# A transformer block on one core: gate and up as Strassen products, in chunks of 256 columns

## The chip, the core and the metric

The kernel runs on one core of a Trainium2 chip. The core's engines run side by side and meet at semaphores: TensorE (PE; its weight loads are PEld), VectorE (DVE), ScalarE (ACT), GpSimd (POOL), and SyncE (SP), which here only issues DMAs. Matmul results go to PSUM, in eight banks of 128 partitions x 512 fp32 values; everything else is in SBUF. The metric is the device time of one execution in microseconds.

## The reference

```python
h = x + A(layernorm(x))            # x: 2048 x 576
out = h + B(layernorm(h))

def A(x):   # softmax attention, 32 heads of 18, no mask
    q, k, v = split_heads(x @ wqkv)
    return merge_heads(softmax(q @ k.T * 18 ** -0.5) @ v) @ wo

def B(x):   # 576 -> 4608 -> 576
    g, u = x @ w_gate, x @ w_up
    return (gelu(g) * u) @ w_down
```

All tensors are fp32.

## The kernel before

**Splits.** Every large product is made of fp16 parts. A matrix is scaled by a power of two and split into `hi` (the fp16 cast) and `lo` (what is left); a product is then x_hi w_hi + x_lo w_hi + x_hi w_lo, added up in PSUM in fp32. With 576 = 4 x 128 + 64, and the hi and lo of the last 64 stacked in one tile of 128 partitions, a gate or up tile takes 14 matmuls (`products`, `accumulate`, L272). `exponents` finds the power of two: VectorE reduces the matrix to `ac` and `am` (L122, L125), TensorE transposes `am` (L129) and later spreads its maximum over all partitions by a matmul with ones (L136), and VectorE makes the scale `p_s_...` from it (L167, L169).

**Attention.** 32 steps n = 0 to 31 (head group n // 4, query block of 512 rows n % 4), 16 key tiles each. `fill` supplies TensorE with other work inside a step, `side` is work that is taken a piece at a time. In the last three steps the output products with `wo` of blocks 0 to 2 (`wo_block`) are the fill; that of block 3 comes after attention. `wo_block` adds x, normalises the rows (`rstd_of` ends with `nb`, `normed`), splits them and turns them by DMA transposes on SyncE's queue (`turn`, L231) into X, from which the MLP reads.

**MLP.** The 4608 columns go in 9 chunks of 512, the 2048 rows in 4 blocks of 512. For a chunk c and a block b, `gate_up(c, b)` makes four column tiles; for each of them 14 gate and 14 up matmuls of 512 columns, gelu on ScalarE into `ga` (L637, three buffers), the product with up on VectorE (L639), the fp16 cast on ScalarE (L640) and the rest `lo` on VectorE (L641). `down(c, b)` multiplies the result with the chunk of `w_down`, 8 groups of 12 matmuls of 288 columns, each added to the rows `nat` by VectorE (L658). The output product of one block is written behind gate and up of the next. While a chunk is computed, the weights of the next are loaded and split (`split_gate_up`: L243 on ScalarE, L244 on VectorE; `split_down`: L622, L623). GpSimd has only memsets in the MLP.

**Order.** In attention TensorE's order is written out (`manual_schedule(engines={PE})`). Elsewhere the framework's scheduler sets it for every engine. PSUM is used as two pairs of banks for gate and up and four single banks for the rest.

## Time and profile before

| | before |
|---|---|
| time, median of 3 runs (range) | 2936.56 us (2935.16 to 2939.13) |
| span of the profiled execution | 2934.4 us |
| TensorE busy | 2786.3 us (95%) |
| VectorE busy | 1941.8 us (66%) |
| ScalarE busy | 1461.2 us (50%) |
| GpSimd busy | 274.5 us (9%) |

The profiled execution is one more execution; its span runs from the first to the last instruction, so what lies around the span in a timed run is not in it. The busy shares are means over two very different stages: attention, up to about 1,600 us, and the MLP behind it.

### The profile page before, as it was taken

The page shows a single profiled execution, that of the slowest core. Times are in us where ns is not written, and L with a number is a line of the kernel's source. Part 1 is how long each engine was busy: PE and PEld are TensorE (multiplying, and loading weights), DVE is VectorE, ACT ScalarE, POOL GpSimd, SP SyncE. Part 2 cuts the span into 40 slices and gives each one's busy share as a digit, 9 for nine tenths or more (in the row PEclk, how much of TensorE's full clock was granted, in tenths as well). Part 3 has the DMA queues.
Part 4 walks back from the last instruction along what each step waited for, and adds up shares of the span by engine and source line. Part 5 has one row for each costly group of instructions (what it writes and reads, how often), then busy time and mean ns, then how long its engine had stood idle before and what let it go on. Part 6 is the DMA issues. An engine that isn't in the chain of part 4 may idle for free.

```text
span 2934.4 us, 43173 instructions
## 1 busy us (share of the span) xinstructions
PE 2786.3 (95%) x17311; PEld 1174.1 (40%) x17311; DVE 1941.8 (66%) x3505; ACT 1461.2 (50%) x1758; POOL 274.5 (9%) x472
## 2 busy tenths in 40 slices
PE   6999999999999999999887999999999999999999
PEld 3532222222222222222323555555555555555555
DVE  7469999999999999999864725252525252524222
ACT  5217888888888888888666312121212121212111
POOL 0002321211112121211001000000000000000000
PEclk9999999999999999999999999999999999999999
DMA  8121000000000000000134301010101010100001
GB/s 221 48 74 57 1 25 1 26 1 19 7 1 25 1 25 1 26 5 30 33 65 101 111 1 53 1 53 1 53 1 53 1 53 1 53 1 1 1 17 49
DMA packets 105433, 95.13 MB, mean 32 GB/s; under 512 B 65872, under 2 KB 79312, under 8 KB 105232
## 3 DMA queue, kind: packets, MB, share of 16 engines
q1 hardware_dynamic: 100256, 83.81, 10.2%
q0 software_dynamic: 4976, 8.56, 1.0%
q8 instruction: 135, 2.21, 0.3%
q14 instruction: 66, 0.54, 0.1%
HBM read 63.70 MB, written 14.16 MB: 27 GB/s over the span
## 4 chain that ended last, share of the span: by engine, by line
PE 54%; DVE 38%; ACT 4%; DMA 2%; issue 1%; POOL 1%; SPq 0%; ACTq 0%; DVEq 0%; POOLq 0%
DVE mx L428 36%; PE pair L272 31%; PE bank L272 16%; PE bank L472 3%; PE bank L425 2%; ACT WK L468 1%; ACT W L243 1%; ACT V L243 1%; PE bank L485 1%; DMA X<-nat 0%; ACT V L622 0%; PE pair L466 0%; POOL rc L492 0%; DMA WK<-in_A_wqkv_dram 0%; ACT W L622 0%
## 5 line engine op out<-in xcount | busy, mean ns | idle before, releaser
L428 DVE TENSOR_REDUCE mx<-bank 128x1 f32<-128x512 f32 x2048 | 1272.1, 683 | 85.6 <-PE bank L425 85.1
L468 ACT ACTIVATE WK<-pair,p_ex_sc 128x1024 f32<-128x1024 f32 x1024 | 1085.5, 1114 | 228.4 <-PE pair L466 225.2
L472 PE MATMUL bank<-WK,V 128*32 128x512 f32 x4096 | 549.4, 608 | 0.1
L272 PE MATMUL pair<-X,V 128*128 128x512 f16 x2240 | 489.0, 379 | 3.1 <-ACT ga L637 3.1
L272 PE MATMUL pair<-X,W 128*128 128x512 f16 x2128 | 469.0, 379 | 1.5 <-ACT ga L637 1.5
L639 DVE SCALAR_TENSOR_TENSOR ga<-pair,p_hsc,ga 128x512 f32<-128x512 f32 x144 | 107.7, 748 | 502.5 <-PE pair L272 502.5
L272 PEld LDWEIGHTS <-WK 128*128 128x128 f16 x3456 | 338.2, 98 | 93.2
L637 ACT ACTIVATE ga<-pair,p_gsc 128x512 f32<-128x512 f32 x144 | 98.8, 686 | 490.1 <-PE pair L272 490.1
L272 PEld LDWEIGHTS <-W 128*128 128x128 f16 x2296 | 222.8, 98 | 275.6 <-issue 20.8
L425 PE MATMUL bank<-W 54*128 54x512 f16 x1024 | 292.3, 382 | 42.0 <-DVE mx L428 14.9
L272 PEld LDWEIGHTS <-V 128*128 128x128 f16 x2240 | 218.5, 98 | 261.8 <-issue 3.9
L425 PE MATMUL bank<-A 54*128 54x512 f16 x1024 | 282.8, 383 | 37.8 <-DVE mx L428 9.9
L640 ACT CAST WK<-ga 128x512 f16<-128x512 f32 x144 | 88.9, 618 | 449.8 <-DVE ga L639 449.8
L658 DVE SCALAR_TENSOR_TENSOR nat<-bank,p_dsc,nat 128x288 f32<-128x288 f32 x288 | 147.9, 515 | 194.9 <-PE bank L272 194.9
L472 PEld LDWEIGHTS bank<-WK,V 128*32 128x32 f32 x4096 | 81.2, 108 | 421.7 <-issue 393.0
L272 PE MATMUL bank<-V,WK 128*128 128x288 f16 x1920 | 239.0, 286 | 0.0
L272 PE MATMUL bank<-W,WK 128*128 128x288 f16 x1536 | 191.4, 286 | 0.0
L492 POOL TENSOR_TENSOR rc<-WK,minus_one 128x16 f32<-128x16 f32 x32 | 93.6, 2926 | 873.6 <-ACT WK L487 873.6
L466 PE MATMUL pair<-W 56*128 56x512 f16 x1024 | 161.1, 379 | 5.7 <-ACT WK L468 5.4
L466 PE MATMUL pair<-A 56*128 56x512 f16 x1024 | 156.8, 380 | 2.8 <-ACT WK L468 2.6
L425 PEld LDWEIGHTS <-W 54*128 54x128 f16 x1024 | 61.8, 93 | 222.5 <-issue 214.6
L641 DVE TENSOR_TENSOR WK<-ga,WK 128x512 f16<-128x512 f32 x144 | 99.3, 689 | 76.3 <-ACT WK L640 76.1
(160 smaller groups left out, 1281.2 us busy)
## 6 DMA issues: line engine op xcount, KB each, us to landing
V<-in_B_w_down_dram SPq DMA_DIRECT2D x9, 1152.0 KB
A<-in_B_w_gate_dram SPq DMA_DIRECT2D x9, 1024.0 KB
A<-in_B_w_up_dram SPq DMA_DIRECT2D x9, 1024.0 KB
qk_hi<-qk SPq DMA_DIRECT2D x36, 128.0 KB
qk_lo<-qk SPq DMA_DIRECT2D x36, 128.0 KB
A<-in_A_x_dram SPq DMA_DIRECT2D x32, 144.0 KB
out_dram<-nat SPq DMA_DIRECT2D x16, 288.0 KB
WK<-in_A_wqkv_dram SPq DMA_DIRECT2D x3, 1152.0 KB
```

The costliest lines, as they stand in the source:

```text
L272: nc.tensor.matmul(dst, a, b, start=(i == 0), stop=(i == len(pairs) - 1))
L425: nc.tensor.matmul(pms[j][:, :TB], Q[r, q0 : q0 + P], K[r, kc * TB : (kc + 1) * TB], start=True, stop=True)
L428: nc.vector.tensor_reduce(mx[:, t, 2 * pr + j, kc : kc + 1], pms[j][:, :TB], axis=AX.X, op=ALU.max)
L466: nc.tensor.matmul(pS[:, j, :TB], K[r, kt * P : (kt + 1) * P], Q[r, qc * TB : (qc + 1) * TB], start=True, stop=True)
L468: nc.scalar.activation(pes[(2 * kt + pr) % NPE], pS[:, :, :TB], AF.Exp, scale=ex_sc)
L472: nc.tensor.matmul(acc[32 * hh : 32 * hh + 32, :TB], Vg[n // NB][:, kt * G4 + hh * VC : kt * G4 + hh * VC + 32], pes[(2 * kt + hh // 2) % ...
L492: nc.gpsimd.tensor_tensor(rc, den, minus_one.to_broadcast([P, TPB * 4]), op=ALU.pow)
L637: nc.scalar.activation(ga, pg[:, :TB], AF.Gelu_apprx_tanh, scale=gsc)
L639: nc.vector.scalar_tensor_tensor(ga, pu[:, :TB], hsc, ga, op0=ALU.mult, op1=ALU.mult)
L640: nc.scalar.copy(hh[:, f], ga)
L641: nc.vector.tensor_sub(hl[:, f], ga, hh[:, f])
L658: nc.vector.scalar_tensor_tensor(nat[:, t, ws], pt[:, :HALF], dsc, nat[:, t, ws], op0=ALU.mult, op1=ALU.add)
```

## The change

**Strassen.** A gate (or up) product of 1,024 rows (a pair of blocks, p = 0, 1) with 256 columns is cut into 2 x 2: rows into two blocks, columns into two tiles of 128, and the 576 of the sum into two halves of 288. The seven products m1 to m7 of sums and differences replace the eight block products. A half of 288 is 2 x 128 + 32, with the parts of the last 32 stacked, so a product takes seven matmuls of 512 columns (`product`). `quad` writes them in the order m3, m2, m5, m4, m1, m7, m6, and combines them into four results: three copies of products on ScalarE and eight additions or subtractions on VectorE that read PSUM. `gate` then has four gelus; `up` has four products with gate on VectorE, four casts on ScalarE and four subtractions for `lo` on GpSimd.

**Rows.** `pair_rows(p)` normalises the rows of two blocks, makes the seven sums and differences, splits them and turns them by two transposes per tile, of 15 and 20 blocks. For p = 0 it is side work of attention's last step; for p = 1 it runs during up(0,0) and down(0,0).

**Weights.** Chunks have 256 columns, so there are 18. `split_mat` makes the sums and differences of the weights as well: scaling and casts on ScalarE, additions and subtractions on GpSimd, in place of VectorE's share. Gate, up and down have an `exponents` call each. `prepare(0)` is side work of attention.

**Order.** The MLP is written in `manual_schedule()` for all engines: each engine does its instructions in program order. `step(cost)` counts time in the program and takes pieces of the side work by the numbers that they yield. The chunk's order is gate(c,p), down of the pair before, up(c,p). The output product of block 3 (`turn_o(3)`, `wo_block(3)`) stands behind gate(0,0). The eight banks are single: acc0 to acc3 for the products, acc4 to acc6 for down, acc7 for `exponents`.

```diff
@@ -54,9 +54,10 @@
     TB = min(512, S)
     NB = S // TB
     TPB = TB // P
-    FT = 4
+    FT = 2
     FC = FT * P
     NCH = DF // FC
+    NPR = NB // 2
     QK = 2 * D
     NG = H // 4
...
                                         apply_absolute_value=True)
-                yield
+                yield 4
         nc.vector.tensor_reduce(am, ac, axis=AX.X, op=ALU.max)
-        yield
-        pt = next(m_ring)
+        yield 9
+        pt = next(e_ring)
         for i in range(n):
             nc.tensor.transpose(pt[0:1, i * P : (i + 1) * P], am[:, i : i + 1], id32)
+        if spread:
+            yield
         a1 = small.tile([1, n], F32, tag=f"a1{n}", name=f"a1_{name}")
         nc.vector.tensor_reduce(a1, pt[0:1, : n * P].rearrange("o (n p) -> o n p", n=n),
                                 axis=AX.X, op=ALU.max)
         nc.vector.tensor_scalar_max(a1, a1, 2.0 ** -60)
-        yield
-        pb = next(m_ring)
+        yield 7
+        pb = next(e_ring)
         nc.tensor.matmul(pb[:, :n], ones[0:1], a1, start=True, stop=True)
+        if spread:
+            yield
...
+    def turn_o(b):
+        for i in range(TPB):
+            nc.sync.dma_start_transpose(OT[:, :, i * P : (i + 1) * P], nat16[:, b * TPB + i])
+
+    def wo_block(b, each=False):
...
-                run(accumulate(pt[:, :HALF], products(slice(t * P, (t + 1) * P), oh, ol, ws)))
+                k = t - b * TPB
+                run(accumulate(pt[:, :HALF], products(slice(k * P, (k + 1) * P), oh, ol, ws,
+                                                      (OT[:, :NK], OT[:, NK], OT[:, NK + 1 :]))))
                 nc.vector.scalar_tensor_tensor(nat[:, t, ws], pt[:, :HALF], u_o, xb,
                                                op0=ALU.mult, op1=ALU.add)
                 yield
             row_stats(nat[:, t], t)
-        rstd_of(b * TPB, TPB)
...
+            if each:
+                rstd_of(t, 1)
+                yield
+        if not each:
+            rstd_of(b * TPB, TPB)
...
+    def pair_rows(p):
+
+        ys, z = rows[p]
+        for v in ys:
+            nc.gpsimd.memset(v[:, :, HALF + 64 : 3 * P], 0.0)
+        for i in range(TPB):
+            t1, t2 = 2 * p * TPB + i, (2 * p + 1) * TPB + i
+            a, b = slice(0, HALF), slice(HALF, D)
+            for k, t, h in ((6, t1, a), (3, t1, b)):
+                nc.scalar.activation(z[:, k], nat[:, t, h], AF.Identity,
+                                     scale=rs[:, t : t + 1], bias=nb[:, t : t + 1])
+            normed(z[:, 0], nat[:, t2, b], t2)
+            normed(z[:, 2], nat[:, t2, a], t2)
+            yield
+            nc.vector.tensor_add(z[:, 1], z[:, 6], z[:, 0])
+            nc.gpsimd.tensor_add(z[:, 4], z[:, 6], z[:, 2])
+            nc.vector.tensor_add(z[:, 5], z[:, 3], z[:, 0])
+            nc.gpsimd.tensor_sub(z[:, 2], z[:, 2], z[:, 0])
+            nc.vector.tensor_sub(z[:, 3], z[:, 3], z[:, 6])
+            for j, k0, k1 in ((1, KA, 7), (0, 0, KA)):
+                y, zz = ys[j], z[:, k0:k1]
+                yield 5
+                nc.scalar.copy(y[:, :, :HALF], zz)
+                yield 5
+                nc.vector.tensor_sub(y[:, :, 3 * P :], zz[:, :, : 2 * P], y[:, :, : 2 * P])
+                nc.vector.tensor_sub(y[:, :, HALF : HALF + 32], zz[:, :, 2 * P :],
+                                     y[:, :, 2 * P : HALF])
+                nc.scalar.copy(y[:, :, HALF + 32 : HALF + 64], y[:, :, 2 * P : HALF])
+                nc.sync.dma_start_transpose(
+                    XP[p][:, NP * k0 : NP * k1, i * P : (i + 1) * P],
+                    y.rearrange("p a b -> p (a b)"))
+            yield
+
+
...
+    def split_mat(src, s167, parts, name):
+
+        h25, l25, h, l = parts
+        l4 = l.rearrange("p k (c n) -> p k c n", c=2)
+        e = yield from exponents([src.rearrange("p (c a) b -> p c (a b)", c=3)], name)
+        s = pow2(e, -1, 267, f"s_{name}")
+        for i in range(2):
+            v = src[:, 3 * i : 3 * i + 3]
+            nc.scalar.activation(v, v, AF.Copy, scale=s)
+            yield
+        f0, f1 = slice(0, P), slice(P, FC)
+        nc.gpsimd.tensor_add(s167[:, 0], src[:, :3, f0], src[:, 3:, f1])
+        nc.scalar.copy(h[:, 3], src[:, :3, f0])
+        yield 5
+        nc.gpsimd.tensor_sub(s167[:, 1], src[:, :3, f1], src[:, :3, f0])
+        nc.scalar.copy(h[:, 4], src[:, 3:, f1])
+        yield 5
+        nc.gpsimd.tensor_sub(s167[:, 2], src[:, 3:, f0], src[:, 3:, f1])
+        yield 5
+        r = slice(64, R3)
+        for k, v in ((3, src[:, :3, f0]), (4, src[:, 3:, f1])):
+            nc.gpsimd.tensor_sub(l4[:, k], v[:, :2], h[:, k, :2])
+            nc.gpsimd.tensor_sub(h[r, k, 2], v[r, 2], h[r, k, 2])
+            yield 5
+        nc.scalar.copy(h[:, :3], s167)
+        for c in range(3):
+            nc.gpsimd.tensor_add(src[:, c], src[:, c], src[:, 3 + c])
+            yield
+        for k in range(3):
+            nc.gpsimd.tensor_sub(l4[:, k], s167[:, k, :2], h[:, k, :2])
+            yield 4
+        nc.gpsimd.tensor_sub(h[r, :3, 2], s167[r, :, 2], h[r, :3, 2])
+        yield 6
+        nc.scalar.copy(h25, src[:, :3])
+        yield 4
+        nc.gpsimd.tensor_sub(l25, src[:, :2], h25[:, :2])
+        nc.gpsimd.tensor_sub(h25[r, 2], src[r, 2], h25[r, 2])
+        yield 6
+        return e
...
+    def split_down(src, c, eg, eu):
+        dh, dl = slots[c % 2][2:]
+        ed = yield from exponents([src], "dn")
         s = pow2(ed, -1, 268, "s_dn")
-        nc.vector.tensor_add(ed, ed, e[:, 0:1])
-        nc.vector.tensor_add(ed, ed, e[:, 1:2])
+        nc.vector.tensor_add(ed, ed, eg)
+        nc.vector.tensor_add(ed, ed, eu)
         dsc = pow2(ed, 1, -262, "dsc")
         for f in range(FT):
-            nc.scalar.activation(dh[:, f], df[:, f], AF.Copy, scale=s)
-            nc.vector.scalar_tensor_tensor(dl[:, f], df[:, f], s, dh[:, f],
+            nc.scalar.activation(dh[:, f], src[:, f], AF.Copy, scale=s)
+            yield
+            nc.vector.scalar_tensor_tensor(dl[:, f], src[:, f], s, dh[:, f],
                                            op0=ALU.mult, op1=ALU.subtract)
+            yield
...
+        yield
+        yield from after("g", need)
+        e = yield from split_mat(a, sums[0], slots[c % 2][0], "g")
+        kept[c, "g"] = pow2(e, 1, -23, "gsc")
+        if not first:
+            load_mat(b, w_up, c, nc.sync)
+            yield 55
+        yield from after("u", need + (c == 1))
+        kept[c, "h"] = pow2(e, -1, 225, "hsc")
+        eu = yield from split_mat(b, sums[1], slots[c % 2][1], "u")
+        kept[c, "u"] = True
...
+    def product(k, xp, parts):
+
+        h25, l25, h, l = parts
+        if k in (2, 5):
+            fs = slice(P, FC) if k == 2 else slice(0, P)
+            wh, wl = h25[:, :, fs], l25[:, :, fs]
+        else:
+            i = {1: 0, 6: 1, 7: 2, 3: 3, 4: 4}[k]
+            wh, wl = h[:, i], l[:, i].rearrange("p (c n) -> p c n", c=2)
+        x = xp[:, NP * XK[k] : NP * (XK[k] + 1)]
+        r = []
+        for c in range(2):
+            r += [(wh[:, c], x[:, c]), (wh[:, c], x[:, 3 + c]), (wl[:, c], x[:, c])]
+        r.append((wh[:R3, 2], x[:R3, 2]))
+        return r
+
+    sides = []
+
+    def step(cost):
+        ghost["now"] += cost
+        for sd in list(sides):
+            while ghost["now"] >= sd[1]:
+                r = next(sd[0], sd)
+                if r is sd:
+                    sides.remove(sd)
+                    break
+                sd[1] += r or 3
+
+    def begin(it):
+        sides.append([it, ghost["now"]])
+        return sides[-1]
+
+    def quad(xp, parts, tmps, out):
+
+        def mm(k):
+            bank = next(single_ring)[:, :TB]
+            ps_ = product(k, xp, parts)
+            for i, (w, x_) in enumerate(ps_):
+                nc.tensor.matmul(bank, w, x_, start=i == 0, stop=i == len(ps_) - 1)
+            step(7)
+            return bank
...
+        c12, c22, c21, c11 = [temp(tmps) for _ in range(4)]
+        m3 = mm(3)
+        nc.scalar.copy(c12, m3)
+        m2 = mm(2)
+        nc.vector.tensor_sub(c22, c12, m2)
+        nc.scalar.copy(c21, m2)
+        m5 = mm(5)
+        nc.vector.tensor_add(c12, c12, m5)
+        nc.scalar.copy(c11, m5)
+        out(0, 1, c12)
+        m4 = mm(4)
+        nc.vector.tensor_add(c21, c21, m4)
+        nc.vector.tensor_sub(c11, m4, c11)
+        out(1, 0, c21)
+        m1 = mm(1)
+        nc.vector.tensor_add(c11, c11, m1)
+        nc.vector.tensor_add(c22, c22, m1)
+        m7 = mm(7)
+        nc.vector.tensor_add(c11, c11, m7)
+        out(0, 0, c11)
+        m6 = mm(6)
+        nc.vector.tensor_add(c22, c22, m6)
+        out(1, 1, c22)
...
+    def up(c, p, hsc, ga, tmps=up_tmps):
+
+        def out(f, b, v):
+            r = ga[f, b]
+            nc.vector.scalar_tensor_tensor(r, v, hsc, r, op0=ALU.mult, op1=ALU.mult)
+            nc.scalar.copy(hh[:, f, b], r)
+            nc.gpsimd.tensor_sub(hl[:, f, b], r, hh[:, f, b])
+
+        quad(XP[p], slots[c % 2][1], tmps, out)
+        ghost["u"] += 1
...
+        for i in range(2 * TPB):
+            t = 2 * p * TPB + i
+            b, tsl = i // TPB, slice(i % TPB * P, (i % TPB + 1) * P)
...
                         run(fill)
+                        turn_o(qc - 1)
                         fill = wo_block(qc - 1)
+                        if qc == 3:
+                            run(side)
+                            side = pair_rows(0)
...
-    e, gsc, hsc = kept[0]
-    for t in range((NB - 1) * TPB, NT):
-        turn(nat16[:, t], t)
-    for _ in wo_block(NB - 1):
-        pass
-    dsc = split_down(0, e)
-    prev = None
-    for c in range(NCH):
-        for b in range(NB):
-            h = gate_up(c, b, gsc, hsc)
-            if prev is not None:
-                down(*prev)
-            prev = (c, b, h, dsc)
-            if b == 0 and c + 1 < NCH:
-                load_gate_up(c + 1)
-                nx = result(split_gate_up(c + 1))
-                ndsc = split_down(c + 1, nx[0])
-        if c + 1 < NCH:
-            (e, gsc, hsc), dsc = nx, ndsc
-    down(*prev)
+    with tc.manual_schedule():
...
+        begin(rest)
+        ga = gate(0, 0, kept[0, "g"], first_gate)
+        for _ in wo_block(NB - 1):
+            step(5)
+        wait_for(1, "g")
+        rows1 = begin(pair_rows(1))
+        up(0, 0, kept[0, "h"], ga, first_up)
+
+        prev = (0, 0)
+        for c in range(NCH):
+            for p in range(NPR):
+                if (c, p) == (0, 0):
+                    continue
+                if (c, p) == (0, 1):
+                    down(*prev, kept[0, "d"])
+                    while rows1 in sides:
+                        step(1)
+                    ghost["rows"] = 1
+                ga = gate(c, p, wait_for(c, "g"))
+                if (c, p) != (0, 1):
+                    down(*prev, wait_for(prev[0], "d"))
+                wait_for(c, "u")
+                up(c, p, kept[c, "h"], ga)
+                prev = (c, p)
+        down(*prev, kept[NCH - 1, "d"])
 
 
```

On VectorE, before, in the MLP where the next chunk's weights are searched for their maximum (`ac_gu`, `am_gu`; `ac_dn`, `am_dn` for the down weights):

```order
L122 TENSOR_REDUCE ac_gu<-A 128x1 x2
L641 TENSOR_TENSOR WK<-ga,WK 128x512
L122 TENSOR_REDUCE ac_gu<-A 128x1 x3
L122 TENSOR_REDUCE ac_dn<-V 128x1
L125 TENSOR_REDUCE am_gu<-ac_gu 128x2
L122 TENSOR_REDUCE ac_dn<-V 128x1 x2
L639 SCALAR_TENSOR_TENSOR ga<-pair_67,p_hsc,ga 128x512
L122 TENSOR_REDUCE ac_dn<-V 128x1
L641 TENSOR_TENSOR WK<-ga,WK 128x512
L125 TENSOR_REDUCE am_dn<-ac_dn 128x1
L639 SCALAR_TENSOR_TENSOR ga<-pair_67,p_hsc,ga 128x512
```

and now, at the end of up(c,0) (L840 and L843 are `quad`'s last two evictions, L861 is up's product with gate, L735 the `lo` of the down weights, L125 and L128 the reductions for the next gate chunk, L826 the first eviction of gate(c,1)):

```order
L735 SCALAR_TENSOR_TENSOR A<-WK,p_s_dn,A 128x576 x2
L840 TENSOR_TENSOR WK<-WK,acc_12926 128x512
L861 SCALAR_TENSOR_TENSOR WK<-WK,p_hsc 128x512
L125 TENSOR_REDUCE ac_g<-W 128x1
L843 TENSOR_TENSOR WK<-WK,acc_12927 128x512
L861 SCALAR_TENSOR_TENSOR A<-WK,p_hsc,A 128x512
L125 TENSOR_REDUCE ac_g<-W 128x1 x2
L128 TENSOR_REDUCE am_g<-ac_g 128x1
L826 TENSOR_TENSOR ga<-ga,acc_12929 128x512
```

The reductions stood between evictions before too; now two instructions for the down weights and the last evictions of up(c,0) are in front of `am_g`, in a fixed order.

On TensorE, before, at the first products behind a chunk's reductions (L129 transposes `am`):

```order
L272 MATMUL bank_71<-W,WK 128x288
L129 MATMUL bank_69<-id_78,am_gu 1x128 x2
L129 MATMUL bank_68<-id_78,am_dn 1x128
L272 LDWEIGHTS V
L272 MATMUL pair_66<-X,V 128x512
```

and now, in gate(c,1) (acc_12926 is the bank of its third product, acc_12927 that of its fourth):

```order
L818 LDWEIGHTS A
L818 MATMUL acc_12926<-V,A 128x512
L132 MATMUL acc_12933<-id_78,am_g 1x128
L818 LDWEIGHTS A
L818 MATMUL acc_12927<-V,A 128x512
```

The transpose of `am_g` now stands between two products of the same quad, and the fourth waits behind it.

On SyncE, before, from the last blocks' turns on (L231; L568 loads x for the output product, L235 to L237 load weights):

```order
L568 DMA A<-in_A_x_dram 128x288 x8
L231 DMA_TRANSPOSE X<-V 128x9x128 x4
L231 DMA_TRANSPOSE X<-nat 128x9x128 x4
L568 DMA A<-in_A_x_dram 128x288
L237 DMA A<-in_B_w_gate_dram 64x512
L568 DMA A<-in_A_x_dram 128x288
```

and now (L569 is `turn_o(3)`, L630 the transposes of `pair_rows(1)`, L577 loads x, L677 and L679 load weights):

```order
L569 DMA_TRANSPOSE V<-nat 128x9x128 x4
L577 DMA V<-in_A_x_dram 128x288 x4
L677 DMA W<-in_B_w_up_dram 128x2x256
L679 DMA W<-in_B_w_up_dram 128x1x256
L677 DMA W<-in_B_w_up_dram 128x2x256
L679 DMA W<-in_B_w_up_dram 128x1x256
L577 DMA V<-in_A_x_dram 128x288 x4
L630 DMA_TRANSPOSE V<-V 128x15x128
L630 DMA_TRANSPOSE V<-WK 128x20x128
```

The transposes of the second pair, of 15 and 20 blocks, stand behind the loads for the last output product; before, block 3's own turns stood there.

## Rows read from the trace of the kernel before

**Rows 1.** The page, its span and the busy row of TensorE.
```profile
span 2934.4 us, 43173 instructions
...
PE 2786.3 (95%) x17311; PEld 1174.1 (40%) x17311; DVE 1941.8 (66%) x3505; ACT 1461.2 (50%) x1758; POOL 274.5 (9%) x472
```

**Rows 2.** Timeline of TensorE, steady part: start us, us, engine, line, operation.
```profile
1903.66 24.34 PE L272 MATMUL pair<-X,V 128*128 128x512 f16 x112
1927.83 11.92 PE L272 MATMUL bank<-W,WK 128*128 128x288 f16 x96
1939.59 0.38 PE L129 MATMUL bank<-id,am_gu 128*1 128x128 f32 x2
1939.81 0.27 PE L129 MATMUL bank<-id,am_dn 128*1 128x128 f32 x1
...
1941.09 0.38 PE L136 MATMUL bank<-a_gu,ones 1*128 1x2 f32 x2
1941.34 0.36 PE L136 MATMUL bank<-a_dn,ones 1*128 1x1 f32 x2
```

**Rows 3.** Windows: stretch, length, busy us by engine (PE, PEld, DVE, ACT, POOL), clock.
```profile
1609.00:1625.00 16.00, 15.82 (x113) 11.94 (x114) 7.47 (x17) 0.00 (x0) 0.00 (x0) 0.87 0.48 96
2300.00:2400.00 100.00, 99.61 (x578) 56.24 (x577) 44.48 (x90) 22.52 (x35) 1.04 (x2) 1.00 0.12 39
```

**Rows 4.** Timeline of TensorE from attention to MLP; in brackets the idle time before.
```profile
1597.78 1.04 PE L272 MATMUL pair<-X,V 128*128 128x512 f16 x4
...
1609.18 15.83 PE L272 MATMUL bank<-W,X 128*128 128x288 f16 x112 [5.39 <-DMA X<-nat]
1624.85 18.94 PE L272 MATMUL pair<-X,V 128*128 128x512 f16 x87
...
1651.84 0.27 PE L129 MATMUL bank<-id,am_dn 128*1 128x128 f32 x1 [3.08 <-DVE am_dn L125]
```

**Rows 5.** Waits of TensorE from 1,600 us on: us in total, times, longest.
```profile
PE pair L272 <- ACT ga L637: 4.7, 9, 1.1
```

**Rows 6.** Groups by line, whole span: count, busy us, mean ns of one.
```profile
L658 DVE SCALAR_TENSOR_TENSOR nat<-bank,p_dsc,nat 128x288 f32<-128x288 f32 x288 | 147.9, 515 | 194.9 <-PE bank L272 194.9
L639 DVE SCALAR_TENSOR_TENSOR ga<-pair,p_hsc,ga 128x512 f32<-128x512 f32 x144 | 107.7, 748 | 502.5 <-PE pair L272 502.5
L641 DVE TENSOR_TENSOR WK<-ga,WK 128x512 f16<-128x512 f32 x144 | 99.3, 689 | 76.3 <-ACT WK L640 76.1
...
L122 DVE TENSOR_REDUCE ac_gu<-A 128x1 f32<-128x512 f32 x90 | 56.5, 667 | 0.0
...
L622 ACT ACTIVATE W<-V,p_s_dn 128x576 f16<-128x576 f32 x16 | 11.0, 761 | 2.9 <-DVE p_s_dn L169 2.9
...
L169 DVE TENSOR_SCALAR p_s_dn<-pi_s_dn 128x1 int32<-128x1 int32 x9 | 1.4, 152 | 0.2
```

**Rows 7.** Groups of GpSimd, shapes apart: count, busy us, mean ns of one.
```profile
L502 POOL CAST nat<-o 128x288 f16<-128x288 f32 x32 | 14.2, 443 | 1.7
...
L551 POOL TENSOR_TENSOR W<-X,W 128x576 f16<-128x576 f32 x4 | 5.1, 1280 | 0.2
...
L505 POOL TENSOR_TENSOR nat<-o,nat 128x256 f16<-128x256 f32 x4 | 2.7, 668 | 0.0
```

**Rows 8.** Timeline of GpSimd at two of those instructions.
```profile
1551.63 0.98 POOL L502 CAST nat<-o 128x288 f16<-128x288 f32 x1
...
1605.14 0.67 POOL L505 TENSOR_TENSOR nat<-o,nat 128x256 f16<-128x256 f32 x1
```

**Rows 9.** Timeline of VectorE at the first of these moments.
```profile
1551.58 0.75 DVE L244 SCALAR_TENSOR_TENSOR V<-A,p_s_gu,V 128x512 f16<-128x512 f32 x1 [1.67 <-ACT V L243]
...
1629.72 0.16 DVE L209 SCALAR_TENSOR_TENSOR nb<-mv,rs 128x4 f32<-128x4 f32 x1
```

**Rows 10.** Transposes by DMA, SyncE's queue: ns min/median/max, first and last start.
```profile
L231 SPq DMA_TRANSPOSE X<-nat x16: 1287/1372/1557, 1430.4 to 1610.4; - x16
```

**Rows 11.** Timeline of ScalarE at the end of attention.
```profile
1580.55 16.19 ACT L468 ACTIVATE WK<-pair,p_ex_sc 128x1024 f32<-128x1024 f32 x16 [2.03 <-PE pair L466]
```

More of the change, by code (lines that the diff above doesn't have):

```diff
@@ L644, in down, with prepare, after @@
-    def down(c, b, h, dsc):
-        hh, hl = h
-        dh, dl = slots[c % 2][4:]
-        for i in range(TPB):
-            t = b * TPB + i
-            tsl = slice(i * P, (i + 1) * P)
+    def prepare(c):
+        first = c == 0
+        a, b, d = (g0, u0, d0) if first else (g1, g1, dn) if c == 1 else (gn, gn, dn)
+        sums = sums0 if first else [sums1, sumsn] if c == 1 else [sumsn] * 2
+        need = 2 * (c - 1)
+        def after(k, last):
+            while not first and ghost[k] < last:
+                yield
+        if first:
+            load_mat(a, w_gate, c, nc.sync)
+            load_mat(b, w_up, c, nc.sync)
+        if c != 1:
+            load_down(d, c, nc.sync)
+        yield
[3 more added lines that the diff above has]
+        if not first:
+            load_mat(b, w_up, c, nc.sync)
+            yield 55
[3 more added lines that the diff above has]
+        kept[c, "u"] = True
+        if c + 1 < NCH and not first:
+            load_mat(gn, w_gate, c + 1, nc.sync)
+        if c == 1:
+            yield from after("rows", 1)
+            load_down(d, c, nc.sync)
+            yield 20
+        yield from after("d", need)
+        kept[c, "d"] = yield from split_down(d, c, e, eu)
@@ new lines, in preparer @@
+    def preparer():
+        for c in range(1, NCH):
+            yield from prepare(c)
+    def product(k, xp, parts):
[12 more added lines that the diff above has]
+        return r
@@ L693, in tile_block @@
         fill = other_products()
-        side = iter(())
         take(fill, 14)
```

161 lines of the change are left out of this document (93 added, 68 removed).

## The prediction

> **What bounds the kernel now.** I read the page's busy rows first, then TensorE's waits from 1,600 us on, then its timeline, and the other engines only where TensorE waits or will wait. The page shows TensorE busy for 95% of a span of 2934.4 us [rows 1]. In the MLP it is the bound: of the 100 us from 2,300 on it is busy for 99.6 at a granted clock of 1.00 (2.4 GHz), with VectorE at 44.5, ScalarE at 22.5 and GpSimd at 1.0 [rows 3]. Its waits on `ga`, the rotating buffer of gelu results, come to 4.7 us in nine times [rows 5]. So a matmul that goes is worth its full pitch, as long as the others keep up. The pitches come from one steady block [rows 2]: 112 gate and up matmuls fill 1903.66 to 1927.83, which is 0.2158 us each, and 96 output matmuls fill 1927.83 to 1939.59, 0.1225 each. Between attention and MLP TensorE isn't the bound: it waits 5.39 us for a transpose and 3.08 for `am_dn` [rows 4].
>
> **What the change removes.** A Strassen product takes 7 matmuls, so gate and up take 18 x 2 x 2 x 49 = 3528 matmuls in place of 9 x 4 x 4 x 28 = 4032: 504 x 0.2158 = **-108.8 us**. The output products stay at 3456 matmuls. The handover's losses of before go as well, because gate(0,0) now stands where TensorE waited: 5.39 and 3.08 [rows 4], the 4.7 on `ga` [rows 5], and the slow clock of the last output product. Its 112 matmuls took 15.83 where 112 x 0.1225 is 13.7, at a mean clock of 0.87, so part of it at 1.2 GHz after the wait [rows 3, 4]: 2.1. Together **-15.3**.
>
> **What it adds on TensorE.** Each `exponents` call puts a transpose and a matmul with ones into TensorE's row. Two transposes took 0.22 (1939.59 to 1939.81) and one such matmul 0.25 (1941.09 to 1941.34) [rows 2], so a call is about 0.36, and the pair of calls of before about 0.83 (three transposes 0.33, two matmuls 0.50). There will be 51 calls in the MLP for nine pairs: 51 x 0.36 - 9 x 0.83 = **+10.9**.
>
> **The handover.** gate(0,0) waits for the transposes of `pair_rows(0)`, which are issued at the end of attention: +1, an estimate. `turn_o(3)` waits for GpSimd's last subtraction. Before, that ended at 1605.81 [rows 8] and TensorE's first output matmul followed at 1609.18 [rows 4], 3.4 later, a transpose of 1.37 [rows 10] and 2.0 of landing. Counted from 1597.78 [rows 4] this is 11.4, against 49 x 0.2158 = 10.6 of cover, 0.8 over; and GpSimd now has one instruction of the weight split in between, 128x576 in 1.28 [rows 7] at most: **+2.1**. At the end of attention ScalarE is full: 16 exponentials without a gap in 16.2 us [rows 11]. Into this go four tiles of 576, 864 and 1,152 elements for `pair_rows(0)`, 4 x 3.4 = 13.7 by L622 [rows 6], and more for `prepare(0)`. TensorE's filler of before leaves room there, so I take **+3**, with -5 and +15 as bounds (all hidden but the handover, all exposed).
>
> **The second pair of blocks.** gate(0,1) needs `pair_rows(1)`, which needs the last `rstd`. From the start of gate(0,0): 10.6, the 2.1, 13.7 of output product, then 4.8 until `nb` (its end at 1629.88 against the product's at 1625.01 [rows 4, 9]) gives 31.2. Behind it VectorE has, in its written order, four tiles of about 4.7 (five of 288 elements, 768, 1,024 and two small ones, at L641's rate of 689 ns for 512 [rows 6]) = 19.0; the evictions of up(0,0), 8 x 0.689 + 4 x 0.748 = 8.5; those of down(0,0), 16 x 0.515 = 8.2; and the exponents of a matrix, 3 x 0.667 and seven small ones of 0.152, 0.2 with the gap between them = 3.4 [rows 6]. That ends at 70.3. The last tile's casts on ScalarE, 864 and 1,152 elements at L622's rate [rows 6], show about 3; the last transpose has 20 blocks, 3.0 by the 1.37 for nine [rows 10], and lands 2.0 later: 78.3. TensorE's own work until then is 26.4 + 10.6 + 11.8 + 0.4 = 49.2. The stall is 29.1, and the clock after it costs twice the 2.1 of the old, shorter gap, 4: **+33.1**. Bounds: 15, where the tiles spread over both engines without queueing, and 45.
>
> **The steady chunks.** Pure TensorE work is 28 x 7 x 0.2158 + 192 x 0.1225 + 3 x 0.36 = 66.9 us for 256 columns. Before it is (4 x (24.17 + 11.76) + 0.83) / 2 = 72.3 for as many [rows 2]. VectorE's list comes to about 55 of it (32 evictions at 0.689, 8 at 0.748, 32 at 0.515, 6 reductions at 0.667, two of 576, `dl`, small ones at 0.152 [rows 6]); GpSimd's to 33. Neither is the bound by its sum, but both are late at two places that the order shows. First, up(c,0)'s second product reads `l25`, the last thing that GpSimd makes of the up weights. Counted from the start of gate(c,0): `am_u`'s product with ones ends at 10.95, VectorE has `p_s_u` at 13.05 behind evictions, ScalarE scales for 1.75 (768 elements twice, at most 1.01 each by L622 [rows 6], whose mean holds a fixed part), and GpSimd's 11.3 follow (eight of 256 at 0.668, and by the step from there to 576 in 1.28 [rows 7] three of 384 at 0.91, one of 512 at 1.16, and 2 for the small ones): 26.1, where TensorE comes to it at 24.6. That is 1.5 per chunk. Second, the transpose of `am_g` stands three products into gate(c,1), at 39.7 with that wait. VectorE starts up(c,0)'s list at 27.8 and has 14.6 of work ahead of `am_g` (evictions, two reductions of 576, two `dl`, three reductions of 512, ten small ones): 42.4, which is 2.7 more. TensorE takes its instructions in order, so everything behind the transpose waits too. The pattern is fixed from chunk 8 on, ten times: 42.5, and I add 4 for chunks 1 to 7, where the side work drifts past less tight places: **+46.5**. Bounds: nothing, if VectorE's instructions overlap enough when they stand close, and twice that.
>
> GpSimd and VectorE now work at the same time, which the MLP of before hardly shows. At the one place where the trace has both, a cast by GpSimd took 0.98 at 1551.63 [rows 8] against a mean of 0.443 [rows 7], while VectorE's L244, with two inputs from SBUF, ran from 1551.58 for 0.75 [rows 9]. The Trainium skill (SBUF — State Buffer, Who interferes with whom) has a rule for this: a VectorE instruction with two SBUF inputs contends with a GpSimd instruction that reads SBUF, and whichever comes first holds the other off. By that rule the trace agrees here, with 0.54 us lost by the second comer. If it held for all ten such instructions of a chunk, and VectorE came second each time, the sum would be that of rival 2 below; by the row alone, GpSimd pays.
>
> **The sum.** 2934.4 - 108.8 + 10.9 - 15.3 + 1 + 2.1 + 33.1 + 46.5 + 3 = 2906.9 of span. The median of the runs is 2936.56, 2.2 above the profiled span, so the forecast is **2909 us**.
>
> **Rivals.** (1) The steady waits are hidden: VectorE's and GpSimd's instructions overlap enough at their pitches for TensorE never to wait in chunks 8 to 17. For it speaks that their sums are 55 and 33 of 67; against it, the two places where the order is strict. Then 2909 - 46.5 = 2863.
> (2) Slower: VectorE and GpSimd hold each other off. Ten VectorE instructions of a chunk have two inputs in SBUF (eight of up's last step, two of `dl`), and GpSimd is busy for half of it. If each costs the chain of `l25` or of `am_g` the 0.54 seen above, that is 5.4 a chunk, 92 in 17: about 3001. It decides from 33 us, 2.0 a chunk, or four of ten meetings on the path. Against it: one meeting is all the trace has, and GpSimd lost there, not VectorE.
> (3) No change: the four product banks turn over too slowly, because a bank is read by ScalarE and then by VectorE before it is free. At 0.4 us for each of the 68 steady quads' handovers, 27 us go, and 2936 is left. Against it: a product takes 1.51, and its two reads about 0.7 each (L641, 0.689 [rows 6], taken for ScalarE's too), with four banks in turn.
> That the change does not cut the matmuls is no rival: the order shows 3528.
>
> **How the numbers follow.** Forecast 0.45, rival 1 0.25, rival 2 0.20, rival 3 0.10. About 0.2% (5.9 us, so 2930.7 to 2942.4) is what a measurement of this kernel can tell from no change. The forecast's own range is 2885 to 2935, from the bounds of the second pair and of the steady waits; 0.42 of its 0.45 lies below the bound of no change. Faster: 0.42 + 0.25 = 0.67. Same: 0.03 of the forecast, 0.07 of rival 3, 0.02 of rival 2 = 0.12. Slower: 0.18 + 0.03 = 0.21. The range reaches down to rival 1 less some of the attention's and the second pair's bounds, 2856, and up into rival 2 to 2955; rival 2 above that and the lowest corner are left out, under 0.2.
>
> **What would show it.** Gate and up at 0.216 a matmul and 3528 of them. One long wait of TensorE, near 29 us, ahead of gate(0,1), ended by a transpose. From chunk 8 on a period near 71.2 us, with TensorE waiting for GpSimd ahead of up(c,0)'s second product and for `am_g` in gate(c,1). A period of 67 shows rival 1; 72 or more with GpSimd's or VectorE's means above those of before shows rival 2. I am wrong if the first product of many quads waits for a bank, or if attention's last two blocks grow by more than 15 us.

## The result, and the profile after

| | before | after |
|---|---|---|
| time, median of 4 runs | 2935.86 us | 2948.89 us (2943.20 to 2951.72) |
| ratio of the times, 95% interval | | 1.0046 (1.0028 to 1.0063) |
| span of the profiled execution | 2934.4 us | 2941.4 us |

The changed kernel is 13 us slower, where 2909 was forecast. Its profiled execution is the fastest of its four; the spans of the others are 2944.8, 2949.5 and 2949.9.

The page of the changed kernel (span, then busy time, share and count by engine):

```profile
span 2941.4 us, 45089 instructions
...
PE 2714.7 (92%) x16906; PEld 1133.3 (39%) x16906; DVE 2398.9 (82%) x4489; ACT 1712.8 (58%) x2144; POOL 886.1 (30%) x1194
```

TensorE has 72 us less to do than in [rows 1], less than the 108.8 of the matmuls that went, and its share fell from 95% to 92%. From the first gate matmul behind attention to the end, first the kernel before, then the changed one (length, TensorE's busy time, and so on by engine):

```profile
1597.78:2934.40 1336.62, 1319.88 (x7665) 750.16 (x7663) 528.27 (x1029) 265.53 (x411) 12.78 (x22) 1.00 0.09 28
```

```profile
1603.55:2941.40 1337.85, 1249.95 (x7246) 708.46 (x7245) 994.96 (x2018) 497.79 (x765) 595.49 (x706) 0.98 0.13 37
```

TensorE works 70 us less there and stands idle 71 us more (87.9 against 16.7). TensorE's waits from 1,590 us on (in total, times, longest), in the place of [rows 5]:

```profile
PE acc L132 <- DVE am_g L128: 29.8, 11, 3.4
PE acc L818 <- DMA V<-WK: 10.7, 1, 10.7
PE acc L279 <- ACT WK L862: 9.5, 2, 8.3
PE acc L818 <- POOL A L720: 6.7, 5, 1.3
PE acc L818 <- POOL W L720: 6.7, 5, 1.3
PE acc L279 <- DVE nat L881: 6.5, 7, 1.8
```

The first, fourth and fifth are the two steady waits: 2.7 us each for `am_g` (L132 is its transpose), 1.34 each for `l25` (L720). The second, and 8.3 of the third and 5.1 of the sixth, lie between gate(0,0) and gate(0,1). TensorE's timeline from gate(0,0) to gate(1,0), which answers to [rows 4]:

```profile
1603.55 10.76 PE L818 MATMUL acc<-X,A 128*128 128x512 f16 x49 [0.56 <-ACT WK L494]
1616.19 5.32 PE L279 MATMUL acc<-W,V 128*128 128x288 f16 x42 [1.88 <-DMA V<-nat]
...
1643.49 4.87 PE L818 MATMUL acc<-X,A 128*128 128x512 f16 x14 [3.41 <-ACT W L827]
1656.61 0.66 PE L279 MATMUL acc<-A,WK 128*128 128x288 f16 x2 [8.26 <-ACT WK L862]
...
1689.21 21.42 PE L818 MATMUL acc<-V,A 128*128 128x512 f16 x91 [10.73 <-DMA V<-WK]
...
1712.52 1.68 PE L818 MATMUL acc<-X,W 128*128 128x512 f16 x7
```

gate(0,1), at 1689.21, is the first work that needs the second pair's rows (V); it comes 85.7 us after gate(0,0). The steady part, two chunks in the place of [rows 2] (X marks gate(c,0) and up(c,0), V the second pair):

```profile
2200.87 7.74 PE L818 MATMUL acc<-X,A 128*128 128x512 f16 x35
...
2227.20 2.77 PE L818 MATMUL acc<-X,A 128*128 128x512 f16 x12 [1.33 <-POOL A L720]
...
2244.62 0.27 PE L132 MATMUL acc<-id,am_g 128*1 128x128 f32 x1 [2.92 <-DVE am_g L128]
2244.73 4.87 PE L818 MATMUL acc<-V,A 128*128 128x512 f16 x14
...
2275.25 7.74 PE L818 MATMUL acc<-X,W 128*128 128x512 f16 x35
...
2317.99 0.27 PE L132 MATMUL acc<-id,am_g 128*1 128x128 f32 x1 [2.52 <-DVE am_g L128]
2318.10 3.19 PE L818 MATMUL acc<-V,W 128*128 128x512 f16 x14
```

The same 14 matmuls take 3.19 us behind a wait of 2.52 and 4.87 behind one of 2.92. The windows say why (granted clock third from the end):

```profile
2244.00:2248.00 4.00, 3.38 (x11) 1.36 (x12) 2.79 (x8) 2.11 (x4) 1.07 (x1) 0.67 0.01 4
...
2320.00:2324.00 4.00, 4.00 (x20) 1.84 (x19) 3.47 (x9) 1.87 (x4) 0.00 (x0) 1.00 0.01 2
```

Behind the first wait part of the stretch runs at 1.2 GHz, a loss of 1.68 us; behind the second none. It isn't the wait's length alone that decides: of the eleven on `am_g`, which take 2.5 to 3.4, four are followed by such a stretch, at 2095, 2170, 2244 and 2463, with 3.41, 2.51, 2.92 and 2.93. A chunk from 2200.87 takes 74.4, the next ones 71.7 and 72.7.

### The profile page after: what moved, and what is told of

Read it like the earlier page. It is cut to its first block, busy times and chain, and to the rows that moved or that the text cites. A ratio compares the mean times of both kernels' runs of the same rounds, so it can differ in the third digit from the quotient of the medians.

```text
span 2941.4 us, 45089 instructions
## 1 busy us (share of the span) xinstructions
PE 2714.7 (92%) x16906; PEld 1133.3 (39%) x16906; DVE 2398.9 (82%) x4489; ACT 1712.8 (58%) x2144; POOL 886.1 (30%) x1194
## 4 chain that ended last, share of the span: by engine, by line
DVE 45%; PE 41%; POOL 5%; issue 3%; ACT 3%; DMA 2%; SPq 0%; POOLq 0%; DVEq 0%; ACTq 0%
DVE mx L435 36%; PE acc L818 19%; PE acc L279 10%; PE pair L279 4%; PE bank L479 2%; PE bank L432 2%; PE bank L279 2%; DVE ac_g L125 1%; ACT WK L475 1%; POOL W L711 1%; DVE ga L861 1%; DVE nat L881 1%; PE bank L492 1%; DMA V<-nat 0%; DVE A L735 0%
## 5 line engine op out<-in xcount | busy, mean ns | idle before, releaser
L279 PEld LDWEIGHTS <-WK 128*128 128x128 f16 x3456 | 337.6, 98 | 114.3 <-ACT WK L862 10.8
L881 DVE SCALAR_TENSOR_TENSOR nat<-acc,p_dsc,nat 128x288 f32<-128x288 f32 x576 | 295.5, 516 | 103.5 <-PE acc L279 101.9
L432 PE MATMUL bank<-W 54*128 54x512 f16 x1024 | 289.9, 381 | 41.2 <-DVE mx L435 13.5
L818 PEld LDWEIGHTS <-A 128*128 128x128 f16 x1764 | 171.6, 98 | 229.0 <-issue 25.6
L279 PE MATMUL acc<-A,WK 128*128 128x288 f16 x1728 | 219.9, 288 | 14.6 <-ACT WK L862 8.3
L279 PE MATMUL acc<-W,WK 128*128 128x288 f16 x1728 | 218.1, 288 | 4.2 <-DVE nat L881 1.4
L818 PE MATMUL acc<-V,A 128*128 128x512 f16 x882 | 201.2, 385 | 12.1 <-DMA V<-WK 10.7
L818 PE MATMUL acc<-X,A 128*128 128x512 f16 x882 | 199.4, 381 | 10.7 <-POOL A L720 6.7
L818 PE MATMUL acc<-X,W 128*128 128x512 f16 x882 | 197.8, 379 | 6.7 <-POOL W L720 6.7
L818 PE MATMUL acc<-V,W 128*128 128x512 f16 x882 | 199.4, 384 | 0.4 <-DVE WK L840 0.4
L863 POOL TENSOR_TENSOR WK<-ga,WK 128x512 f16<-128x512 f32 x74 | 88.3, 1193 | 220.8 <-ACT WK L862 142.2
L432 PEld LDWEIGHTS <-A 54*128 54x128 f16 x1024 | 60.3, 93 | 214.6 <-issue 208.0
```

The lines of the kernel that those rows point to most:

```text
L279: nc.tensor.matmul(dst, a, b, start=(i == 0), stop=(i == len(pairs) - 1))
L432: nc.tensor.matmul(pms[j][:, :TB], Q[r, q0 : q0 + P], K[r, kc * TB : (kc + 1) * TB], start=True, stop=True)
L818: nc.tensor.matmul(bank, w, x_, start=i == 0, stop=i == len(ps_) - 1)
L863: nc.gpsimd.tensor_sub(hl[:, f, b], r, hh[:, f, b])
L881: nc.vector.scalar_tensor_tensor(nat[:, t, ws], pt[:, :HALF], dsc, nat[:, t, ws], op0=ALU.mult, op1=ALU.add)
```

## The experiments

Ratios are to the kernel before on the same chip; the changed kernel's is 1.0046, and 0.001 is 2.9 us. Differences between two of them are known to about 4 to 7 us.

**One of the steady waits: `l25`.** In `split_mat`:

```diff
+        nc.scalar.copy(h25, src[:, :3])
+        yield 4
+        nc.gpsimd.tensor_sub(l25, src[:, :2], h25[:, :2])
...
         for k in range(3):
             nc.gpsimd.tensor_sub(l4[:, k], s167[:, k, :2], h[:, k, :2])
...
-        nc.scalar.copy(h25, src[:, :3])
-        yield 4
-        nc.gpsimd.tensor_sub(l25, src[:, :2], h25[:, :2])
```

> Only the order inside the weights' split changes: the parts for the second and fifth product (h25, l25) are made before the lo parts of the first, sixth and seventh, so l25 is ready about 2.6 us sooner, against a wait of 1.34. Theory (each of the two waits of a chunk is a cost of its own): the 13.4 us of waits on l25 in ten chunks go, the waits on am_g stay at 29.8, the time falls by 11 to 15 us. Rival (VectorE's list sets the pace, the wait only moves): the waits on am_g grow by what is gained, the time stays within 4 us.

1.0043 (1.0028 to 1.0058): no gain that can be told from noise. Neither reading was right. The waits on `l25` are gone, those on `am_g` are as they were (first row), but the mean clock of 2,200 to 2,800 fell to 0.98 (second):

```profile
PE acc L132 <- DVE am_g L128: 30.2, 11, 3.4
```

```profile
2200.00:2800.00 600.00, 576.74 (x3307) 324.71 (x3305) 455.51 (x921) 228.71 (x349) 278.45 (x333) 0.98 0.10 31
```

0.99 is the changed kernel's value there. The clock was lower in all four executions: 0.980 to 0.983 over the span, against 0.986 and 0.987 for the changed kernel. The early chunks lost as well: chunks 1 to 5 take 354.8 in place of 343.2, with two new waits of 3.4 and 2.3 on ScalarE's evictions and low clock behind them.

**The other one: the transpose of `am_g` two products later.**

```diff
-        yield 9
+        yield 23 if name == "g" else 9
...
-            yield 55
+            yield 41
```

> Only the place of the transpose of am_g changes: two products later in TensorE's row, with the up split's start held where it was. Theory (the wait is one of place, and the low clock behind it goes with it): the 29.8 us of waits on am_g go, so does the low clock in four of the steady chunks (1.7 us each), the time falls by 30 to 38 us. Rival (VectorE is late as a whole): waits for banks or for evictions take its place, the time falls by less than 12 us.

0.9954 (0.9938 to 0.9971), 27 us below the changed kernel: a little less than the theory's 30 to 38, and far more than the rival's 12. The waits on `am_g` are gone, those on `l25` stay (13.3), and the clock of that stretch is 1.00. A new wait of up to 0.7 on ScalarE's first copy of a quad (7.0 in ten) is what the rival has. A steady chunk takes 70.0, some 71.0.

**Both.**

> The two edits together. Theory: the steady chunk falls to TensorE's own work, 67.2 us, the time falls by 43 to 52 us against the changed kernel and ends some 35 us below the kernel before. Rival (VectorE at its limit): a chunk stays above 69 us and the time falls by less than 30 us.

0.9921 (0.9907 to 0.9936), 37 us below the changed kernel and 23 below the one before: between the theory's 43 to 52 and the rival's 30. A steady chunk takes 68.5 to 69.5, where the theory had 67.2. In the early chunks two waits of 3.8 came in, where ScalarE's cast of `h25` (L713) stood in its row ahead of an eviction (L827) and waited for GpSimd:

```profile
1898.41 0.83 ACT L713 CAST A<-W 128x768 f16<-128x768 f32 x1 [5.06 <-POOL W L711]
1899.15 0.58 ACT L827 COPY ga<-acc 128x512 f32<-128x512 f32 x1
```

```profile
1899.78 4.87 PE L818 MATMUL acc<-V,W 128*128 128x512 f16 x14 [3.79 <-ACT ga L827]
```

**Does the low clock cost by itself?** Twelve matmuls without use fill the wait:

```diff
         pt = next(e_ring)
+        if spread and name == "g" and ghost["g"] >= 13:
+            for i in range(12):
+                nc.tensor.matmul(pt[:, :TB], id16, XP[0][:, 0], start=True, stop=True)
```

> The changed kernel with 12 matmuls of no use (an identity with rows that are in place, into the bank of the exponents) ahead of each of the eleven transposes of am_g that waited, 2.6 us of work in a wait of 2.5 to 3.4. The transposes come no sooner. Theory (the wait costs its length and then a stretch at 1.2 GHz, in some executions after more of the waits than in others): the stretches at the low clock behind these waits go, 1.7 us each for the 4 in the profile, up to 11 in slower executions, the time falls by 5 to 12 us and the runs lie closer together. Rival (the low clock costs nothing that the wait does not): the time stays within 3 us.

> The same 12 matmuls in the kernel where l25 is made first, whose profile shows ten low stretches behind its waits on am_g. Theory: 10 x 1.7 = 17 us come off its 2947, to 2926 to 2933, so that the 13 us forecast for l25 alone are there after all. Rival: within 4 us of 2947.

1.0019 (1.0009 to 1.0029) and 0.9997 (0.9988 to 1.0006): 8 and 13.5 us below the same kernels without the filler, each known to 5 to 6 us; both are what the theory said. The same window of the two, where the changed kernel had 0.99 and the kernel with `l25` made early 0.98:

```profile
2200.00:2800.00 600.00, 587.91 (x3431) 333.41 (x3428) 453.76 (x930) 231.62 (x352) 280.54 (x338) 1.00 0.10 30
```

```profile
2200.00:2800.00 600.00, 600.00 (x3495) 340.32 (x3492) 462.32 (x944) 235.73 (x359) 285.04 (x341) 1.00 0.11 32
```

None of the low stretches behind `am_g` is left in either. Not all of the 8 us is the clock's: counted from its chunk's start, the transpose of `am_g` stands where it stood in seven of the eleven chunks, 1.0 sooner in three and 1.0 later in one.

In the second TensorE is busy all through that window and a chunk takes 70.2. Making `l25` early gains something as soon as the clock holds: 1.0019 to 0.9997 is 6.5 us. In the traces of the two, chunks 6 to 16 became 13.7 shorter, as the theory of the first run had it, and chunks 1 to 5 were 10.7 longer by the new waits there. The runs did not lie closer together (2929.9 to 2941.3), so that part was wrong.

**Meetings of GpSimd and VectorE.**

```diff
+            if ghost["u"] < 1:
-            nc.gpsimd.tensor_sub(hl[:, f, b], r, hh[:, f, b])
+                nc.gpsimd.tensor_sub(hl[:, f, b], r, hh[:, f, b])
```

> Leaves out GpSimd's subtraction that makes the lo part of the hidden activations, from the second quad of up on (the output products read what stands there). In the changed kernel VectorE's product of up with gate, both inputs from SBUF, has a mean of 0.96 us on ga against 0.748 for L639 of before, which read PSUM. Theory (meetings of GpSimd and VectorE cost a few tenths each, so that they are a small part of the wait on am_g): that mean falls to 0.75 to 0.80, the wait from 2.7 to about 1.9, the time falls by 6 to 16 us. Rival (they are the main cost, 5 us a chunk): it falls by more than 35.

The run leaves out GpSimd's four subtractions of each up but the first. 0.9958 (0.9941 to 0.9975), 26 us, between the two. VectorE's L861 over the whole span, first in the changed kernel, then here:

```profile
L861 DVE SCALAR_TENSOR_TENSOR ga<-WK,p_hsc,ga 128x512 f32<-128x512 f32 x71 | 70.6, 994 | 1.7
```

```profile
L861 DVE SCALAR_TENSOR_TENSOR ga<-WK,p_hsc,ga 128x512 f32<-128x512 f32 x71 | 56.3, 793 | 1.7
```

0.2 us went from each, and the waits on `am_g` fell:

```profile
PE acc L132 <- DVE am_g L128: 17.8, 11, 3.4
```

That is 1.6 a wait in place of 2.7; a steady chunk takes 70.7, and the clock of 2,200 to 2,800 is 1.00, so the 26 us hold the low clock as well as the shorter waits.

**The second pair's rows.**

```diff
-    XP = [view(X, 0, (7 * NP, TB)), view(V, 0, (7 * NP, TB), F16)]
+    XP = [view(X, 0, (7 * NP, TB)), view(X, 0, (7 * NP, TB))]
...
-        rows1 = begin(pair_rows(1))
+        rows1 = begin(iter(()))
```

> Leaves out the sums, differences and transposes of the second pair of row blocks: the products of the second pair read those of the first. Theory (the stall ahead of gate(0,1), with TensorE's low clock around it, is the price of this step): gate(0,1) starts some 23 us after the output product's end in place of 57, the time falls by 32 to 40 us, the steady chunks stay as they are. Rival (the stall is made by the evictions of up(0,0) and down(0,0) and the weights' split, which stay): the time falls by less than 15 us.

0.9941 (0.9926 to 0.9956), 31 us, just under the theory's 32 to 40. Gate(0,0) and gate(0,1):

```profile
1601.99 10.76 PE L818 MATMUL acc<-X,A 128*128 128x512 f16 x49 [0.56 <-ACT WK L494]
...
1659.68 21.37 PE L818 MATMUL acc<-X,A 128*128 128x512 f16 x98
```

57.7 in place of 85.7: the step costs 28 in the trace. From the output product's end to gate(0,1) it is 29, not the 23 expected: the waits that are left between gate(0,0) and gate(0,1) come to 7.8, 4.3 of them on the casts and subtractions of up(0,0).

**The moved output product.**

```diff
-        ga = gate(0, 0, kept[0, "g"], first_gate)
         for _ in wo_block(NB - 1):
             step(5)
+        ga = gate(0, 0, kept[0, "g"], first_gate)
```

> The changed kernel with the last block's output product ahead of gate(0,0), as before. Theory (the second pair's rows behind the output product set when gate(0,1) can start, and both orders have the output product wait for the same transposes): gate(0,1) starts within 3 us of where it does now, and the time stays within 4 us. Rival (the move hides the wait for the transposes, as forecast): the time rises by 8 to 12 us.

1.0068 (1.0051 to 1.0085): 6 us slower by the ratios, with an uncertainty as large, so the time doesn't decide between the two. The trace speaks for the rival: it has the wait for the transposes that the move hides, and gate(0,1) at 1695.98 after an equal end of attention, 6.8 later:

```profile
1617.14 15.57 PE L279 MATMUL acc<-W,V 128*128 128x288 f16 x112 [14.20 <-DMA V<-nat]
```

The output product starts at 1617.14 against 1616.19: with the move, the 10.8 of gate(0,0) are done during that wait. At gate(0,1) 6.8 of them are left.

**Seven for eight.**

```diff
-        m6 = mm(6)
+        bank = next(single_ring)[:, :TB]
+        for k in (6, 6):
+            ps_ = product(k, xp, parts)
+            for i, (w, x_) in enumerate(ps_):
+                nc.tensor.matmul(bank, w, x_, start=i == 0, stop=i == len(ps_) - 1)
+        step(7)
+        m6 = bank
```

> The changed kernel with the sixth product of each quad computed twice into the same bank: 504 matmuls more, as many as the change took away, with no further eviction. Theory (TensorE is the bound but waits on am_g and l25 give some of it back): 504 x 0.216 = 109 us, less up to 25 that VectorE's lead takes from the waits on am_g and from the low clock: the time rises by 84 to 105. Rival (VectorE and GpSimd set the pace of the changed kernel): it rises by less than 60.

1.0329 (1.0311 to 1.0346): 83 us above the changed kernel by the ratios (80 by the medians), at or just under the theory's lower end. The missing 26 to 29 are mostly the waits on `am_g`, which fell by 16, and the clock, since one low stretch behind them is left of four (5 us):

```profile
PE acc L132 <- DVE am_g L128: 13.7, 11, 2.7
```

**Better versions of the handover.** All three have both mended waits and the cast of `h25` one product later (`yield 7`; the yields behind it are shortened, so that the rest stays in place). The other lines move down(0,0) behind gate(0,1), in the second and the third, and write the rows as a whole ahead of up(0,0), in the second alone:

```diff
+        yield 7
         nc.scalar.copy(h25, src[:, :3])
...
-        rows1 = begin(pair_rows(1))
+        run(pair_rows(1))
...
-                    down(*prev, kept[0, "d"])
...
-                if (c, p) != (0, 1):
-                    down(*prev, wait_for(prev[0], "d"))
+                down(*prev, wait_for(prev[0], "d"))
```

> The run with both edits, with the cast of h25 written one product later and nothing else. Theory (its two waits of 3.8 us behind ScalarE and their low clock are what the run with the rows first gained): 8 to 12 us below 2911, as the run with the rows first. Rival (the rows first gained it): within 3 us of 2911.

> The two edits of the run with both, with the cast of h25 written one product later (there it made ScalarE wait for GpSimd ahead of evictions, 3.8 us twice), and the second pair's rows written as a whole ahead of up(0,0), so that down(0,0) can stand behind gate(0,1) as in every other chunk. Theory (the second pair's rows are late because VectorE has evictions of up(0,0) and down(0,0) in between): gate(0,1) starts 58 to 66 us after gate(0,0) in place of 86, with 11.8 us of output products still to come, so the handover gains 8 to 16 us, the two waits of 3.8 go as well, and the time falls to 2888 to 2902. Rival (the rows' own chain over ScalarE, GpSimd and the transposes sets it, and evictions only fill its gaps): gate(0,1) starts later than 72 us, and the time stays above 2903.

> Both mended waits with the cast of h25 one product later, the second pair's rows among the evictions of up(0,0) as in the changed kernel, and down(0,0) behind gate(0,1). With the rows written first their chain took 29 us over VectorE, GpSimd, ScalarE and the transposes, of which VectorE worked 20; evictions of up(0,0) fit into its gaps. Theory (the chain sets gate(0,1), down(0,0) no longer delays it): gate(0,1) starts 68 to 74 us after gate(0,0) with all of up(0,0) done and down(0,0) still to come, the time falls 4 to 10 us below the run with the rows first. Rival (evictions in program order hold up the chain tile by tile): gate(0,1) starts later than 78 us and nothing is gained.

0.9924 (0.9909 to 0.9939), 0.9894 (0.9875 to 0.9913), 0.9927 (0.9912 to 0.9941). Moving the cast alone gave nothing measurable, as its rival said, though the waits of 3.8 went. With the rows first:

```profile
1607.04 10.77 PE L819 MATMUL acc<-X,A 128*128 128x512 f16 x49 [0.56 <-ACT WK L494]
...
1669.97 7.45 PE L819 MATMUL acc<-X,A 128*128 128x512 f16 x21 [28.18 <-ACT W L825]
1677.26 6.22 PE L819 MATMUL acc<-V,A 128*128 128x512 f16 x28
```

Gate(0,1) starts 70.2 after gate(0,0) and the median is 2903.1, both between the readings: the rows' own chain takes 29 us, with gaps in which VectorE waits for ScalarE (1.9 in the last tile), and ScalarE for GpSimd (1.6) and for the transposes out of its single buffer (1.6). With the rows among the evictions it starts 79.6 after gate(0,0) and nothing is gained, as that run's rival said. This version has a wait of another kind, since the transpose of `am_u` now stood in TensorE's row ahead of gate(0,1) and its reductions behind the rows:

```profile
PE acc L132 <- DVE am_u L128: 18.2, 1, 18.2
PE acc L819 <- DMA V<-WK: 15.2, 1, 15.2
```

The rows first is the best version, 31 us below the kernel before. What its 8 us over the cast alone come from is not settled: their intervals overlap a little, and the profiled executions (spans of 2905.2 and 2903.3) can't show it: one is the slowest of its four, the other the fastest.

## Why the prediction was wrong

The forecast of the span was 2906.9; it came to 2941.4. By stretches of the trace, forecast against measured:

| stretch | forecast | measured |
|---|---|---|
| start of gate(0,0) | 1601.8 | 1603.55 |
| from there to gate(0,1) | 78.3 | 85.7 |
| to gate(1,0), with the low clock behind the stall | 25.5 | 23.3 |
| chunks 1 to 7 (to 2200.87) | 472.3 | 488.4 |
| chunks 8 to 16 (to 2852.46) | 640.8 | 651.6 |
| the rest | 88.2 | 88.9 |

- **The matmuls (-108.8)**: right in place and nearly in size. 504 more cost about 80 us, and most of the rest came out of the waits.
- **The two steady waits (42.5 in ten chunks)**: right in place, releaser and total (29.8 in eleven and 13.4 in ten chunks, 43.2). But the 2.7 for `am_g` was luck: errors cancelled. Counted from the start of the chunk at 2275.25, VectorE has `am_g` at 42.7 (forecast 42.4) and TensorE comes to it at 40.2 (39.7). I took VectorE's instructions at durations without GpSimd beside them; with GpSimd's subtractions gone `am_g` is there at 41.7, so the list was priced 0.7 too long and the 1.0 that GpSimd adds was left out. Without it the eleven waits are 1.6 on average, not 2.7.
- **The step that failed: TensorE's own time, in two terms of the sum.** From gate(0,0) on, the sum lets TensorE's work fall by 96 us (-108.8 and +10.9; for the clock -2.1 and +4). It fell by 70. TensorE's idle time there is 87.9, not far above the 81.2 that the forecast comes to (16.7 before, less 13.2 of the old waits, and 2.1, 29.1 and 46.5).
  - *The clock.* "The steady chunks", +46.5, priced each wait at its own length, and the low clock stood behind the one long stall and nowhere else (+4). Summed over the stretches at 1.2 GHz, TensorE's work lost 14.0 us (half of its busy time in them): 5.6 up to gate(1,0), 6.7 in the four stretches behind the waits on `am_g`, 1.7 at the end. The filler shows that this clock costs time by itself: 8 us in the changed kernel, and 13.5 where only the `l25` wait had been removed.
  - *The pure work of a chunk, 66.9.* The chunk from 1919.73 has no wait, and its clock is 1.00:

```profile
1919.73:1987.64 67.91, 67.78 (x398) 38.73 (x397) 52.75 (x111) 24.94 (x39) 33.55 (x40) 1.00 0.11 33
```

It takes 67.9, and 1.0 more in each of 17 chunks is 17 us. Half of that is the exponents (+10.9): the trace has 0.11 for a transpose, 0.31 for its ones product, and 0.1 by which the matmul ahead of the ones product takes longer than its neighbours, 0.52 a call and not 0.36. In all that is 26.4, against 8.6 before: 17.8. The rest is the pitch of the matmuls (0.2165 against 0.2159, 2 us) and other seams. No run tried this term by itself.
- **Chunks 1 to 7** were to be nearly free of waits (+4). They are up to chunk 5 (67.9 to 70.0 each); chunks 6 and 7 already wait for `am_g`, 3.4 and 2.5, both with the low clock behind it.
- **The handover**: the output product waits 1.9 for `turn_o(3)` (2.1). Up to gate(0,1) TensorE is idle for 32.2, where 31.2 was forecast (2.1 and 29.1). But it isn't one long wait: 10.7 of it lie ahead of gate(0,1), ended by a transpose, and 21.5 in the output product, up(0,0) and down(0,0). With the work of these pieces at the low clock (4.0 lost) the stretch is 7.4 longer; behind gate(0,1) the clock cost 1.6, not 4. In total the step cost 31 us, near the 33.1 forecast. The attention's end was 1.8 short: ScalarE makes TensorE wait for 12.4 us there, against 5.4 before, while the waits on VectorE's maxima fell from 5.9 to 1.9.
- **Rival 2** had the right sign, but its price was too high and only part of its mechanism is there. VectorE loses 0.2 us in each L861, not 0.54. What GpSimd loses is not clear: L711 has a mean of 0.744 against 0.668 for L505 [rows 7], but even its shortest takes 0.717. In time it is 26 us, inside the forecast's waits and the low clock behind them. By the rule of the Trainium skill (SBUF — State Buffer, Who interferes with whom), a VectorE instruction with two inputs in SBUF contends with a GpSimd instruction that reads SBUF, and one with at most one, outside its two-port modes, does not. The traces agree: L861, with two, falls from 0.994 to 0.793 when GpSimd's subtractions are gone, and L826, with one of its inputs in PSUM, stays at 0.686 and 0.687.
- **Rivals 1 and 3**: the two waits are not hidden (rival 1), and banks cost little, L840 1.1 us in three (rival 3).

The rest to the median is 5.3: the four executions spread over 8.5 us, and the profiled one is the fastest. The two slowest have the lower mean clock (0.986 against 0.987); that they have more of the low stretches is likely, but no trace of them was taken.

So where did the 124 us go that were taken out (108.8 of matmuls, 15.3 of the old handover)? From gate(0,0) to the end it is 1337.9 us, against 1336.6 from 1597.78 [rows 4] before: all of it was spent again. Of these 125 us the trace puts 84 on idle time that the forecast's base did not have (32 in the handover, 43 in the two steady waits, the other 9 in small waits), 14 on the clock, 18 on the exponents, and 9 on the pitch and on the ends of rows of matmuls ahead of waits, which are not measured one by one. The end of attention adds 5.8. The runs confirm the large parts: 31 us without the second pair's rows, 37 with both steady waits mended (their clock with them, less the new waits that came in). Of all this the steady waits were not needed: an earlier cast and a later transpose in the weights' preparation give back 37 us, and the change is then 23 us faster than the kernel before.
